# Attention and a gated feed-forward in one kernel: the odd 64 tokens of the first token group move into the second group's product buffers

## The chip, the cores and the metric

The kernel runs on one core of a Trainium2 chip. The metric is the device time of one execution in microseconds (us), the median of several runs.

## The reference, cut to what matters

```python
# q, k, v: (8, 8, 576, 64), float32.  x: 4608 tokens of 512 channels
q_s = softmax(q, axis=-1)               # over the 64 channels of a head
k_s = softmax(k, axis=2)                # over the 576 positions
kv  = einsum('bhsd,bhse->bhde', k_s, v)
x   = einsum('bhsd,bhde->bhse', q_s, kv)   # then (4608, 512)
a, b = x @ w1, x @ w2                   # 512 -> 1024 each
h   = (a * b) @ w3                      # 1024 -> 1024
out = h @ w_out                         # 1024 -> 512
```

No non-linearity stands between `w3` and `w_out`, so the kernel multiplies those two once (`W3O`, 1024 x 512) and the token work is: attention, the products `a` and `b`, their elementwise product, and a third product with `W3O`.

## The kernel before, in words

**Units of work.** Attention runs batch by batch (8 batches of 576 tokens, each in two halves of four heads). Its result is written, transposed, into `xt` (channels on partitions, tokens along the row). The 4608 tokens are cut into six groups for the feed-forward: `GROUPS = [(0, 576), (576, 576), (1152, 1024), (2176, 640), (2816, 1024), (3840, 768)]`. A group has 8 feature blocks `fb` of 128 rows of the 1024 features; each ends in one buffer `ab` (128 x 1024, float16) that holds `a * b` for the group's tokens. There are 18 `ab` buffers, and they are also used at the start for casting `w3` and `w_out`.

**Group 0** takes `plain`: for each `fb` the tokens are cut in two parts (`cut`: 256 and 320 tokens), and `plain_part` issues, for each part, four matmuls for `a` (tasks `pa0`, `pa1`, two each) and four for `b` (`pb0`, `pb1`) at line 591, a copy of `a` to float16 (`pac`, ScalarE or VectorE, line 344) and a multiply (`pm`, VectorE, line 605). **Groups 1 to 5** take `wino`, which gets the two products out of seven half-size products (tasks `x1` to `x4`, `v1`, `v2`, `w`, two matmuls each at line 648) with sums made before (`t_comb`, line 626) and after (line 672, and a multiply at line 699).

**The third product** is `s2`: for a tile of 128 tokens, eight matmuls of 512 columns accumulate over the features (line 739, four tasks of two), then an eviction (line 725 or 727) and two stores of 64 tokens each. Groups 0 and 1 hold 576 tokens, four tiles and 64 tokens more. Those two remainders share one output tile in `s2_ends` (line 759): sixteen matmuls whose stationary operand has 64 columns, eight for the upper half of the output from group 0's buffers and eight for the lower half from group 1's. So all eight `ab` buffers of group 0 are read once more when group 1 is done. Group 4 makes most of its third product by `s2_halves`, the same seven-product scheme (line 836); it needs combinations of `W3O` (`t3_comb`, line 790), which lie in two `st` buffers.

**Loads.** All inputs come through nine `st` buffers (128 x 1152, float32), issued by SyncE (line 310) in the order of the schedule: first `w3` and `w_out`, then q, v and k of the first batch mixed with the rest of them, then `w1` and `w2` in eight pieces, then the other batches. A load waits until the buffer's last reader is done.

**What sets the order.** Every step is a `Task` with a number. Three tables at the head of the file fix everything: `ORDER` (the order in which tasks are emitted, and with it the order on each engine; entries such as `('ps', 7, 9)` are nine filler matmuls that keep TensorE running, line 931), `SLOTS` (which buffer of its pool each use takes) and `ENGS` (which engine takes a task that could run on several). They are the output of a planner that is not part of the file.

Of the kernel before, what the change touches and what calls it, by code (L numbers as in the profile page):

```python
# [18 lines left out]
    ('ps', 7, 9), 6, 12, 4, 14, 1, 10, 3, 2, 96, 0, 97, ('ps', 7, 2), 120, 121, ('ps', 7, 2), 88, 89,  # L19
    ('ps', 7, 3), 90, 128, 98, 5, 129, ('ps', 7, 4), 122, 8, 130, 68, 123, 112, 131, 99, 91, 69, 113, 124,  # L20
    15, 114, 100, 7, 80, 92, 9, 115, 13, 116, 72, 81, 132, 82, 73, 70, 74, 83, 133, 11, 104, 84, 16, 101,
    93, 17, 75, 152, 18, 76, 20, 153, 105, 77, 106, 85, 125, 154, 107, 71, 108, 155, 109, 19, 156, 78, 157,
    134, 144, 21, 86, 142, 145, 94, 79, 126, 143, 87, 102, 140, 95, 117, 146, 135, 110, 103, 147, 160, 136,
    118, 158, 137, 127, 111, 148, 22, 150, 119, 149, 24, 162, ('ps', 7, 3), 151, 23, 164, 139, 163, 138,
    171, 168, ('ps', 7, 4), 141, 173, 170, 159, 169, 161, 172, 25, 165, 180, 166, 484, 167, 508, 182, 174,
    177, 176, 472, 178, 496, 179, 478, 175, 490, 502, 466, 509, 473, 510, 485, 479, 181, 486, 467, 497,
    468, 474, 503, 498, 491, 183, 511, 480, 481, 475, 469, 470, 505, 188, 499, 500, 512, 501, 482, 476, 27,
    483, 504, 506, 190, 487, 26, 471, 493, 513, 488, 28, 186, 538, 477, 492, 494, 30, 189, 507, 526, 550,
    31, 527, 539, 29, 528, 551, 540, 514, 489, 36, 556, 532, 495, 184, 515, 552, 533, 516, 529, 194, 534,
    553, 520, 191, 517, 521, 541, 535, 192, 518, 557, 522, 530, 212, 519, 542, 536, 214, 523, 537, 559,  # L30
    524, 543, 554, 531, 185, 544, 525, 547, 1186, 213, 1200, 558, 545, 196, 560, 215, 548, 202, 1207, 216,
    1208, 204, 203, 217, 1201, 200, 555, 1187, 205, 1193, 546, 1194, 206, 197, 561, 1188, 549, 1202, 201,
    207, 1209, 218, 1210, 219, 187, 1189, 198, 1203, 193, 220, 199, 210, 221, 195, 222, 1190, 1204, 32,
    223, 1211, 34, 208, 225, 211, 1195, 1192, 224, 1196, 209, 37, 232, 235, 229, 38, 234, 233, 236, 237,
    226, 33, 230, 231, 598, 227, 1205, 568, 228, 562, 583, 1197, 1213, 581, 563, 596, 582, 566, 1191, 597,
    587, 584, 585, 567, 600, 564, 586, 611, 569, 570, 601, 588, 599, 571, 603, 565, 626, 589, 602, 35, 604,
    590, 573, 591, 42, 605, 627, 572, 592, 593, 574, 606, 244, 594, 613, 630, 607, 612, 595, 576, 1206,
    575, 608, 628, 631, 609, 615, 578, 629, 616, 632, 610, 579, 633, 246, 641, 577, 618, 580, 634, 614,
    617, 39, 619, 643, 243, 636, 642, 635, 658, 620, 621, 1212, 638, 644, 623, 242, 637, 645, 40, 671, 624,
    646, 656, 673, 622, 672, 648, 657, 639, 647, 649, 1228, 247, 640, 238, 675, 677, 625, 676, 660, 674,  # L40
    1229, 650, 651, 245, 661, 678, 653, 288, 1242, 654, 679, 1243, 652, 286, 655, 663, 680, 662, 248, 664,
    681, 683, 239, 249, 682, 1244, 684, 284, 1230, 43, 665, 1221, 659, 1235, 254, 289, 666, 685, 668, 240,
    1222, 669, 256, 250, 287, 252, 670, 1236, 41, 296, 290, 1237, 667, 1199, 291, 251, 1223, 257, 1198,
    1224, 255, 1238, 1225, 1231, 258, 241, 1239, 1227, 1245, 259, 1232, 292, 297, 1226, 294, 253, 264, 295,
    298, 265, 293, 1214, 281, 266, 285, 1215, 267, 280, 299, 271, 268, 44, 273, 260, 300, 262, 272, 47,
    261, 301, 1216, 270, 263, 283, 45, 1217, 269, 1233, 282, 274, 277, 306, 275, 1241, 279, 307, 278, 1246,
    48, 690, 308, 276, 1218, 304, 46, 309, 302, 305, 52, 313, 310, 303, 315, 705, 54, 311, 312, 720, 314,
    688, 319, 316, 321, 750, 317, 318, 692, 320, 691, 686, 722, 721, 707, 687, 330, 696, 693, 694, 706,
    724, 689, 695, 709, 723, 711, 710, 331, 697, 735, 708, 698, 712, 699, 700, 725, 726, 713, 701, 702,
    328, 727, 703, 737, 728, 714, 715, 704, 337, 756, 716, 736, 717, 1182, 730, 751, 729, 739, 718, 754,  # L50
    740, 731, 741, 755, 752, 738, 719, 322, 732, 753, 742, 335, 782, 733, 362, 743, 49, 757, 1240, 744,
    745, 734, 765, 1248, 746, 758, 767, 1247, 766, 329, 747, 323, 780, 50, 748, 769, 61, 759, 760, 749,
    770, 771, 761, 781, 795, 358, 1183, 768, 772, 784, 324, 783, 786, 773, 785, 1270, 796, 775, 336, 326,
    1271, 774, 787, 762, 1184, 776, 53, 788, 799, 1234, 763, 797, 1277, 789, 800, 1278, 359, 338, 327, 790,
    325, 777, 55, 791, 792, 1220, 332, 802, 764, 333, 801, 798, 803, 1249, 778, 1250, 793, 1256, 805, 779,
    334, 1298, 339, 804, 340, 1299, 1251, 806, 1219, 807, 1257, 808, 1279, 794, 1272, 341, 809, 1258, 1273,
    1280, 1274, 1263, 363, 1264, 1265, 1281, 342, 343, 1283, 1266, 360, 345, 57, 1300, 344, 361, 1267,
    1259, 1252, 1260, 1269, 346, 378, 1268, 347, 348, 352, 379, 1275, 353, 812, 349, 1301, 351, 381, 59,
    354, 829, 380, 1276, 350, 355, 810, 861, 357, 830, 831, 60, 811, 356, 859, 814, 832, 860, 813, 833,
    815, 816, 834, 863, 364, 818, 862, 844, 817, 836, 819, 835, 1302, 837, 821, 366, 1284, 838, 820, 845,  # L60
    822, 839, 56, 396, 1285, 840, 1282, 848, 823, 841, 1303, 1286, 849, 842, 846, 51, 1253, 365, 824, 843,
    864, 1304, 826, 889, 825, 865, 1254, 827, 851, 866, 828, 852, 850, 867, 1291, 847, 400, 1185, 854, 853,
    1287, 868, 869, 855, 874, 870, 856, 875, 1292, 890, 1288, 1293, 857, 891, 1290, 367, 858, 871, 878,
    1262, 872, 893, 398, 880, 879, 1289, 894, 895, 892, 373, 876, 58, 881, 877, 896, 882, 1312, 873, 897,
    368, 1294, 883, 371, 369, 919, 898, 899, 372, 920, 901, 886, 402, 923, 902, 1305, 1295, 887, 904, 903,
    374, 924, 370, 884, 905, 1319, 399, 888, 375, 921, 900, 1306, 885, 376, 1255, 908, 401, 397, 910, 926,
    909, 925, 922, 927, 1320, 403, 911, 1321, 928, 912, 377, 929, 404, 906, 405, 930, 409, 931, 914, 913,
    1313, 407, 932, 916, 915, 395, 1333, 917, 1314, 907, 406, 1326, 933, 1327, 918, 410, 1328, 1322, 408,
    1261, 1315, 1323, 411, 1334, 412, 394, 1335, 1316, 385, 382, 387, 1329, 384, 386, 413, 383, 391, 388,
    392, 393, 998, 390, 389, 414, 999, 63, 415, 1330, 1318, 1000, 416, 62, 1336, 417, 1001, 66, 421, 418,  # L70
    64, 1307, 422, 419, 420, 1308, 1325, 423, 936, 427, 424, 1324, 428, 938, 425, 426, 1317, 1015, 429,
    934, 939, 1013, 1332, 443, 940, 935, 1296, 953, 1014, 937, 942, 1002, 941, 943, 1017, 1003, 1016, 945,
    944, 954, 946, 1005, 1004, 947, 1006, 948, 438, 1007, 957, 950, 949, 958, 1008, 436, 951, 1010, 960,
    1009, 67, 952, 955, 1297, 1011, 961, 959, 439, 963, 434, 1018, 1019, 1309, 956, 1020, 1337, 1012, 962,
    968, 1021, 1339, 1045, 437, 969, 965, 1331, 1340, 431, 1022, 1043, 65, 1023, 430, 964, 1310, 1025,
    1342, 445, 966, 1028, 1311, 1044, 1026, 972, 967, 974, 440, 973, 1024, 1047, 1029, 970, 1027, 1046,
    1048, 1030, 971, 435, 975, 441, 444, 1050, 1032, 976, 446, 983, 1033, 989, 977, 432, 1049, 1031, 1344,
    442, 1051, 978, 447, 980, 984, 1052, 1035, 448, 981, 1338, 987, 1036, 1034, 979, 988, 1053, 433, 1037,
    990, 982, 1038, 1054, 449, 991, 450, 1039, 993, 1346, 992, 1040, 994, 451, 1341, 995, 453, 985, 452,
    1345, 1041, 454, 457, 455, 1055, 996, 456, 1343, 458, 986, 460, 459, 463, 1092, 462, 1056, 461, 1077,  # L80
    464, 1062, 997, 465, 1064, 1042, 1063, 1356, 1058, 1078, 1079, 1057, 1093, 1068, 1059, 1376, 1060,
    1081, 1348, 1066, 1082, 1352, 1096, 1067, 1349, 1084, 1357, 1353, 1069, 1065, 1360, 1355, 1080, 1070,
    1358, 1350, 1361, 1072, 1097, 1363, 1354, 1359, 1099, 1364, 1351, 1362, 1347, 1380, 1365, 1366, 1071,
    1368, 1061, 1367, 1085, 1374, 1369, 1073, 1074, 1373, 1375, 1083, 1075, 1378, 1370, 1377, 1087, 1100,
# [151 lines left out]
def kernel(  # L236
# [11 lines left out]
    nc = tc.nc  # L248
# [716 lines left out]
```

The softmax here doesn't subtract the row's maximum and nothing guards it: scores larger than these inputs give would overflow.

## Time and profile before

| | |
|---|---|
| median of 6 runs | 231.44 us (230.94 to 232.38) |
| profiled execution | 232.04 us, of which the span in the profile is 230.2 us |
| granted TensorE clock | 1.0 throughout |
| TensorE matmul busy | 220.1 us (96%) |
| VectorE busy | 183.5 us (80%) |
| ScalarE busy | 142.1 us (62%) |
| GpSimd busy | 100.9 us (44%) |
| bytes moved | 50.92 MB, of which 38.80 MB are read from HBM |

The profiled execution is one run; 1.8 us of its time lie outside the span. Busy times of matmuls are modelled ends: a matmul's row lasts from its start to its result, and the next one starts long before that, so what a matmul costs is read from the distance of starts (a stretch of x matmuls in the chain, divided by x), not from its mean duration.

### The profile page before, as it was taken

How to read it: one execution, taken by the hardware profiler on the slowest of the kernel's cores; microseconds unless marked ns; L12 is line 12 of the kernel's file. 1: busy time of each engine (PE TensorE's matmuls, PEld its weight loads, DVE VectorE, ACT ScalarE, POOL GpSimd, SP SyncE). 2: the span in 40 equal slices, each digit the busy share in tenths (PEclk: the TensorE clock that was granted, in tenths of full speed). 3: DMA queues.
4: the chain of work that ended last, by engine and by line, in shares of the span. 5: the costliest groups of instructions: out<-in, count | busy, mean ns of one | idle time of the engine just before them, and what ended most of it. 6: DMA issues, size and time to landing. Idle time of an engine off the chain costs nothing.

```text
span 230.2 us, 5284 instructions
## 1 busy us (share of the span) xinstructions
PE 220.1 (96%) x1971; PEld 124.5 (54%) x1971; DVE 183.5 (80%) x392; ACT 142.1 (62%) x289; POOL 100.9 (44%) x84
## 2 busy tenths in 40 slices
PE   7899999999999999999999989999999999999992
PEld 2454448865676564444445656543444367766640
DVE  0432975789999988999967989999999999889820
ACT  2335965768768998777527658765799474354021
POOL 3322545584064990197940368800299920310000
PEclk9999999999999999999999999999999999999999
DMA  6999997980997669819786976669885702124556
GB/s 238 393 405 391 390 387 253 381 325 16 370 374 309 159 234 351 324 29 341 197 190 170 279 276 171 128 106 298 277 213 152 78 0 48 23 68 92 116 132 164
DMA packets 32888, 50.92 MB, mean 221 GB/s; under 512 B 11744, under 2 KB 12000, under 8 KB 32864
## 3 DMA queue, kind: packets, MB, share of 16 engines
q1 hardware_dynamic: 31504, 48.57, 66.6%
q10 hardware_dynamic: 1360, 2.03, 3.7%
q8 instruction: 15, 0.25, 0.4%
q14 instruction: 9, 0.07, 0.1%
HBM read 38.80 MB, written 9.44 MB: 210 GB/s over the span
## 4 chain that ended last, share of the span: by engine, by line
PE 76%; DVE 9%; DMA 8%; ACT 3%; SPq 2%; issue 1%; DVEq 0%; ACTq 0%
PE ps L648 38%; PE ps L739 19%; PE ps L591 7%; PE ps L836 5%; DMA st<-in_q_dram 4%; DMA st<-in_moe_w_out_dram 4%; PE ps L556 2%; PE ps L511 2%; DVE ds L459 2%; SPq L310 2%; DVE tt L626 2%; DVE cc L672 1%; PE ps L485 1%; DVE eq L469 1%; DVE xt L344 1%
## 5 line engine op out<-in xcount | busy, mean ns | idle before, releaser
L672 DVE TENSOR_TENSOR cc<-ps,uu 128x512 f16<-128x512 f32 (+3 forms) x120 | 65.1, 569 | 2.8 <-PE ps L648 0.7
L344 ACT COPY uu<-ps 128x512 f32<-128x512 f32 (+3 forms) x107 | 50.5, 501 | 25.8 <-PE ps L648 14.7
L699 POOL TENSOR_TENSOR ab<-cc,cc 128x512 f16<-128x512 f16 (+3 forms) x25 | 23.1, 927 | 70.4 <-DVE cc L672 59.6
L739 PE MATMUL ps<-W3O,ab 128*128 128x512 f16 (+1 forms) x224 | 53.4, 372 | 0.0
L648 PE MATMUL ps<-tt,wc 128*128 128x512 f16 (+3 forms) x240 | 52.1, 334 | 0.3
L648 PEld LDWEIGHTS <-wc 128*128 128x128 f16 x320 | 30.9, 98 | 25.6 <-DVE tt L626 1.4
L648 PE MATMUL ps<-xt,w 128*128 128x512 f16 (+3 forms) x160 | 36.6, 334 | 0.8 <-ACT osb L725 0.7
L648 PEld LDWEIGHTS <-w 128*128 128x128 f16 x240 | 22.6, 97 | 18.4 <-issue 2.1
L739 PEld LDWEIGHTS <-ab 128*128 128x128 f16 x224 | 21.4, 98 | 20.1 <-issue 0.6
L469 POOL TENSOR_TENSOR eq<-eq,ds 128x1152 f16<-128x1152 f16 x13 | 28.0, 2154 | 5.8 <-DVE ds L466 4.2
L725 ACT ACTIVATE osb<-ps 128x512 f32<-128x512 f32 (+1 forms) x24 | 13.3, 566 | 22.5 <-PE ps L739 19.9
L459 DVE TENSOR_REDUCE ds<-eq 128x9 f32<-128x576 f16 x32 | 23.4, 742 | 4.2 <-ACT eq L455 4.2
L672 DVE TENSOR_TENSOR ab<-ps,cc 128x512 f16<-128x512 f32 (+3 forms) x40 | 22.4, 566 | 1.8 <-PE ps L648 0.6
L455 ACT ACTIVATE eq<-st 128x576 f16<-128x576 f32 x32 | 21.6, 686 | 1.8 <-DMA st<-in_q_dram 1.7
L434 ACT ACTIVATE ek<-st 128x576 f16<-128x576 f32 x32 | 21.0, 686 | 1.9 <-DMA st<-in_k_dram 1.6
L344 ACT CAST xt<-ps 128x320 f16<-128x320 f32 (+7 forms) x46 | 15.2, 398 | 9.4 <-PE ps L556 9.1
L648 PE MATMUL ps<-xt,wc 128*128 128x512 f16 (+3 forms) x80 | 20.2, 334 | 0.0
L648 PE MATMUL ps<-tt,w 128*128 128x512 f16 (+3 forms) x80 | 19.7, 334 | 0.0
L591 PE MATMUL ps<-xt,w 128*128 128x320 f16 (+1 forms) x128 | 16.2, 286 | 0.0
L377 PE MATMUL ps<-ab,ab 128*128 128x512 f16 x64 | 14.8, 379 | 0.4 <-ACT ab L344 0.3
L591 PEld LDWEIGHTS <-w 128*128 128x128 f16 x128 | 12.3, 98 | 3.6 <-issue 0.2
L344 POOL CAST ab<-st 128x1024 f16<-128x1024 f32 x6 | 6.2, 1041 | 15.0 <-DMA st<-in_moe_w_dram 9.1
(76 smaller groups left out, 257.4 us busy)
## 6 DMA issues: line engine op xcount, KB each, us to landing
st<-in_q_dram SPq DMA_DIRECT2D x16, 576.0 KB, 5.8
st<-in_v_dram SPq DMA_DIRECT2D x16, 576.0 KB, 7.5
st<-in_k_dram SPq DMA_DIRECT2D x16, 576.0 KB, 6.4
st<-in_moe_w_dram SPq DMA_DIRECT2D x16, 512.0 KB, 9.0
out_dram<-osb SPq DMA_DIRECT2D x56, 128.0 KB, 3.8
st<-in_moe_w_out_dram SPq DMA_DIRECT2D x4, 512.0 KB, 7.6
out_dram<-osb ACTq DMA_DIRECT2D x14, 128.0 KB, 2.4
out_dram<-osb ACTq DMA_DIRECT2D x3, 64.0 KB, 2.6
```

Source lines behind the costliest of these rows:

```text
L344: {"DVE": nc.vector.tensor_copy, "POOL": nc.gpsimd.tensor_copy, "ACT": nc.scalar.copy}[eng](out=o, in_=i)
L377: nc.tensor.matmul(pp.tile, lhsT=wT.tile[:, gt * P:(gt + 1) * P], rhs=wo[i][1].tile[:, (gt % 2) * C:(gt % 2 + 1) * C], start=(gt == 0), st ...
L434: nc.scalar.activation(out=ek.tile[:, :, j, :], func=AF.Exp, in_=vk(bk.tile)[:, j].rearrange("p (r d) -> p r d", r=RK))
L455: nc.scalar.activation(out=eq.tile[:, :, j, :], func=AF.Exp, in_=vq(bq.tile)[:, j].rearrange("p (r d) -> p r d", r=RK))
L459: nc.vector.tensor_reduce(out=ds.tile[:, 0, j], axis=AX.X, op=ALU.add, in_=eq.tile[:, :, j, :])
L469: {"POOL": nc.gpsimd, "DVE": nc.vector}[e].tensor_tensor(out=eq.tile, in0=eq.tile, op=ALU.mult, in1=ds.tile[:, 1].rearrange("p j r -> p r ...
L591: nc.tensor.matmul(ps.tile[:, 0:m], lhsT=w[qt][:, ct, fo:fo + P], rhs=x[:, ct, lo:lo + m], start=(ct == 0), stop=(ct == 3))
L648: nc.tensor.matmul(ps.tile[:, 0:h], lhsT=lhs(c), rhs=rhs(c), start=first and c == 0, stop=c == 1, skip_group_check=not first)
L672: return lambda: nc.vector.tensor_tensor(out=dst(), in0=ps.tile[:, 0:h], in1=other.tile[:, 0:h], op=op)
L699: {"POOL": nc.gpsimd, "DVE": nc.vector}[e].tensor_tensor(out=ab.tile[:, 0:h], in0=c11.tile[:, 0:h], in1=c21.tile[:, 0:h], op=ALU.mult)
L725: nc.scalar.activation(out=o(), in_=i(), func=AF.Copy, scale=ISC)
L739: nc.tensor.matmul(po.tile[:, :w], lhsT=ab_buf[(g, ft)].tile[:, tb * P:(tb + 1) * P], rhs=W3O[:, ft, m * w:(m + 1) * w], start=(ft == 0), ...
```

## The change

The last 64 tokens of group 0 are no longer a remainder of their own. `plain` cuts group 0 in 512 and 64 tokens, and the product of the 64 is written to columns 576 to 639 of the `ab` buffer that group 1 will use for the same feature block. That buffer is taken already in `plain`, and `wino` of group 1 picks it up. Group 1 then has five full tiles of 128 rows for the third product, of which the last stores half to group 0's tokens; `s2_ends` is gone.

Two more things change. The combinations of `W3O` for group 4 move out of the `st` buffers: two into a new buffer `twx`, two into the first halves of the `w2` weights after their last use; the `st` pool shrinks from nine buffers to eight. And `ORDER`, `SLOTS` and `ENGS` are new tables throughout, since the tasks and the pools are others. (`XCUT` is empty, and the general forms of `rest` and `rows` give the same tiles for groups 2 to 5 as before.)

```diff
+    twx = konst.tile([P, 2, 4, C // 2], F16, name="twx")
-    tiles("st", 9, [P, 2 * RK * D], F32)
+    tiles("st", 8, [P, 2 * RK * D], F32)
...
     def plain(g, fb):
-        ab = buf("ab")
+        ab = ab_buf.get((g, fb)) or buf("ab")
...
         cut = [n * m // parts // 64 * 64 for m in range(parts + 1)]
+        if ENDS and g == 0:
+            ab_buf[(1, fb)] = buf("ab")
+            cut = [0, n - 64, n]
...
     def plain_part(g, fb, qt, fo, ab, lo, m):
+        end = ENDS and g == 0 and lo
+        to, at = (ab_buf[(1, fb)], GROUPS[1][1]) if end else (ab, lo)
+
         def mul():
-            nc.vector.tensor_tensor(out=ab.tile[:, lo:lo + m], in0=pb.tile[:, 0:m], in1=a16.tile[:, 0:m],
+            nc.vector.tensor_tensor(out=to.tile[:, at:at + m], in0=pb.tile[:, 0:m], in1=a16.tile[:, 0:m],
                                     op=ALU.mult)
...
     def wino(g, fb, tb, ts):
-        c11, c22, c21, ab = buf("cc"), buf("cc"), buf("cc"), buf("ab")
+        c11, c22, c21 = buf("cc"), buf("cc"), buf("cc")
+        ab = ab_buf.get((g, fb)) or buf("ab")
...
     def s2(g, tb, parts=1):
...
+        ends = ENDS and g == 1 and at[1] == GROUPS[1][1]
+        if ends:
+            tok = (tok[0], GROUPS[0][0] + GROUPS[0][1] - 64)
...
-    def s2_ends(g0, g1):
-        po, osb = buf("ps"), buf("osb")
...
-                    for m, g in enumerate((g0, g1)):
-                        e = GROUPS[g][1]
-                        nc.tensor.matmul(
-                            po.tile[64 * m:64 * m + 64, :], lhsT=ab_buf[(g, ft)].tile[:, e - 64:e],
-                            rhs=W3O[:, ft], start=(ft == 0), stop=(ft == N_FT - 1))
...
     def t3_comb():
-        bufs = [buf("st"), buf("st")]
...
+        spent = [t for t in plan.tasks if t.name[0] in ("pb0", "wc0", "wc2")]
...
-        if g == 1 and GROUPS[g][1] % P:
-            s2_ends(0, 1)
...
+        if g == 1 and ENDS:
+            rest = [0, 1, 2, 3, (GROUPS[1][1] - 64, GROUPS[1][1])]
```

## The prediction

> **What bounds the kernel now.** I read the page's slices first, to see which engine is never idle and until when the start lasts.
>
> ```profile
> PE   7899999999999999999999989999999999999992
> DVE  0432975789999988999967989999999999889820
> DMA  6999997980997669819786976669885702124556
> ```
>
> A slice is 5.8 us. The DMA engines are full through the first six slices, TensorE nearly always, VectorE from the ninth on. A full digit for TensorE does not say that matmuls follow each other without holes, so next I read the chain of waits in order of time, and take matmul spacing from its long pieces.
>
> ```profile
> 14.36 8.82 DMA st<-in_q_dram
> ...
> 32.58 0.72 PE ps L591 x4
> ...
> 33.84 14.48 PE ps L591 x118
> ...
> 49.99 3.88 PE ps L739 x18
> ...
> 84.07 0.98 PE ps L759 x8
> ...
> 87.83 0.64 DVE xt L344
> ...
> 225.69 0.60 ACT osb L725
> ```
>
> The chain has four parts. Until 32.58 us loads and the first batch's attention; from there to 225.69 us TensorE work (193.1 us); then 4.5 us of eviction and store. In the middle, at 76 to 92 us, the chain runs over VectorE pieces: TensorE waits there in small bits, while it passes from group 1 to group 2.
>
> The spacing of matmuls: 3.88 / 18 = 0.2156 us for 512 columns with a full 128x128 stationary operand; 14.48 / 118 = 0.1227 for the equal mixture of 256 and 320 columns in group 0. The narrowest full one is the transpose at line 485, 128 columns. The forms of TensorE, and one stretch of the timeline:
>
> ```profile
> L591 PE MATMUL ps<-xt,w 128*128 128x320 f16 x64 | 11.8, 299 | 0.0
> L591 PE MATMUL ps<-xt,w 128*128 128x256 f16 x64 | 9.7, 272 | 0.0
> L485 PE MATMUL ps<-ident,eq 128*128 128x128 f16 x72 | 5.7, 219 | 0.4 <-DVE eq L469 0.4
> L759 PE MATMUL ps<-W3O,ab 128*64 128x512 f16 x16 | 2.1, 385 | 0.0
> ```
>
> ```profile
> 83.39 0.68 PE L485 MATMUL ps<-ident,eq 128*128 128x128 f16 x9
> ...
> 86.05 0.11 PEld L648 LDWEIGHTS <-w 128*128 128x128 f16 x2
> ```
>
> Nine transposes take 0.68 us, the last one's own 0.219 included: (0.68 - 0.219) / 8 = 0.0576 us each. Between 128 and 512 columns the spacing thus grows by (0.2156 - 0.0576) / 384 = 0.00041 us a column. With these spacings the counts of the forms table after 32.58 us come to: 432 of 512 columns 93.1; 112 of 384, 176 of 320, 112 of 288 and 192 of 256 together 77.2; line 759 2.0; 54 transposes 3.1; seven batches of 72 small ones at line 511, 0.70 each, 4.9; 15 sets of line 556 at some 0.40, 6.0. That is 186.3 of 193.1 us: only about 7 us are lost to waits after the start. That is the ceiling for any better order.
>
> **The change part by part.** *Group 0's products.* 128 matmuls of 256 and 320 columns (128 x 0.1227 = 15.7 us) become 64 of 512 (64 x 0.2156 = 13.8) and 64 of 64 columns, each with a full weight load. No row shows 64 columns with a full load. Lower bound: the line through the two rows gives 0.0576 - 64 x 0.00041 = 0.031 us. Upper bound: the 128-column row, 0.0576, since the load is the same. The sum is 15.8 or 17.5 us, so +0.1 or +1.8. I take 0.031, because the last row above shows two full weight loads within 0.11 us while one takes 0.098: they follow each other after some 0.012 us, so the load is not what spaces matmuls.
>
> The Trainium skill ("TensorE: Matmul & The Clock Gate", Back-to-back issue gap) speaks against this change: it holds that in a stream of weight loads and matmuls both set the spacing, and gives about 81 ns at 128 columns where this trace has 57.6. By the page's figure the 64 narrow matmuls would take 5.2 us, an estimate, and the change would cost over 3 us here; the row decides, and the sum goes without it.
>
> *Its evictions.* The same number, 16 copies and 16 multiplies. VectorE's multiply took 0.475 and 0.415 us for 320 and 256 columns, 0.681 for 512; for 64 the nearest rows are 0.224 (the 128x64 multiply at line 522) on VectorE and 0.222 (the 128x64 cast) on ScalarE. Per block 0.905 for 0.890, eight times 0.015 = 0.1 us on VectorE, which is 8.0 of 10 us busy in 40 to 50 us. Nothing on the path; +0.1 if that cover were gone.
>
> *The shared tile.* Sixteen half-width matmuls run in pairs: 8 in 0.98 us, 16 in 2.0. Eight full ones take 8 x 0.2156 = 1.7. Gain 0.2 us, on TensorE's path: nearly nothing, since the halves already ran side by side.
>
> *Fillers.* 20 instead of 27, all before the first product, where TensorE waits: 0.
>
> *The load buffer.* At the start the DMA engines are full (1.04 and 1.05 of 16 engines in 10 to 30 us, some 390 GB/s). The first `w1` piece remains the 19th load, behind the same bytes. Eight buffers could leave a hole of at most one buffer, 0.59 MB / 390 GB/s = 1.5 us; on the other side the last q load goes up by one place (one `w3` piece, 0.52 MB, 1.3 us earlier), and the chain above runs through it. I take 0, between -1.3 and +1.5. Later the reads have room: 38.8 MB are 99 us at that rate, and what stands behind a late load on SyncE's queue are stores of third-product tiles, which nobody but their own four buffers awaits. `t3_comb` now waits for the last use of `w2`; group 4's third product, its only reader, comes 90 us after `w2`'s loads, and `pb0` and the `wc` sums are over by then.
>
> *The `ab` buffers, and the order.* Before, group 0's eight buffers are held until its remainder is read (line 759, ending 85 us); with group 1's eight only 2 of 18 are free for group 2, and all of group 1's third product stands ahead of group 2's first product on TensorE. After, group 0's buffers are free after its four tiles. The new order uses that: behind group 2's first product stand two whole tiles of group 1 (16 matmuls, 3.45 us) that TensorE can do while VectorE makes `xt` and the sums of line 626. What was lost there is read from the window:
>
> ```profile
> 76.20:92.00 15.80, 15.52 (x267) 8.31 (x265) 14.10 (x34) 14.60 (x32) 9.14 (x7) 1.00 0.82 267
> ```
>
> Its 267 matmuls by their spacings: 35 of 512 columns 7.5, 36 transposes 2.1, line 759 2.0, 144 small ones 1.4, four sets of line 556 1.5 (at 0.37, the pieces that waited least), 4 of 288 columns 0.5: 15.0 of 15.8 us; at the 0.22 that two pairs of 256 columns need, 14.4. So 0.8 to 1.4 us can be had here. A stall that goes lets VectorE be late next: it is 14.1 of 15.8 us busy here, and its work is the same. The other passages (120 to 134, 150 to 161, 177 to 186 us) have new orders too, with 1.7 us of group 3's tiles behind group 4's first product where 1.3 were; I see no sign for either side there and put -1.0 to +1.5 (the holes counted at 177 to 186 us come to about 0.8, the largest of the three). For order and buffers together I take -1.2, the middle of what this passage holds and nothing for the others, between -1.4 - 1.0 = -2.4 and +1.5.
>
> Sum: +0.1 - 0.2 - 1.2 = -1.3 us. The profiled execution (232.04, of which span 230.2) would become 230.7; it was 0.6 above the median 231.44, so on the median's scale 230.1.
>
> **The rivals.** *Same time:* VectorE gets the freed time and is late next. For it: VectorE is at 9 or more tenths for most of 45 to 200 us, and its work by counts and rows changes by about 1 us of 175 (seven evictions of third-product tiles leave it, copies at the start come). Then only +0.1 - 0.2 remains: 231.4. *Slower:* the 64-column products are spaced by their weight load, at 0.0576 instead of 0.031 us, 64 x 0.027 = +1.7, with no gain elsewhere: 233.0. It decides from a spacing of some 0.05 us on, where 64 x 0.019 = 1.2 eats the gain. For it: no row shows a full load with so little work behind it; against it: the two loads in 0.11 us. A late load at the start, with the first product at 34 us instead of 32.6, would give the same sign. *It does not do what it says:* for TensorE's work this is nearly so, 0.2 us, and it is in the sum.
>
> **How the numbers follow.** Faster by over 0.3% (0.7 us, about what a measurement of this kernel can tell from no change): the gain at the passage holds, and spacing stays under 0.045: 0.47. Within it: 0.18. Slower, by the narrow products, the load buffers or a passage that the new order makes worse: 0.35. All gains at their ends give 231.44 - 1.3 - 2.4 - 0.1 = 227.6, all losses 231.44 + 1.8 + 1.5 + 1.5 = 236.2; neither is likely whole. The range takes the likeliest case's lower half and the slower rival: 228.4 to 233.3.
>
> **What would show it.** Line 591's 64-column form: starts 0.03 or 0.06 us apart. The first product at 32.6 us, within 1 us. Line 739's rows among line 648's where group 2 begins, and holes of TensorE there under 0.5 us. It would be wrong if the first product came after 34 us, if line 591's work took over 17 us, or if the 7 us of holes after the start grew.

## The result and the profile after

| | before | after |
|---|---|---|
| median | 231.35 us (37 runs) | 232.84 us (18 runs, 231.50 to 234.65) |
| ratio | | 1.0065, 95% interval [1.0046, 1.0083] |
| profiled execution | 232.04 us, span 230.2 | 233.09 us, span 231.3 |

The change makes the kernel slower by about 1.5 us; 230.1 was forecast. The page's slices of the kernel after, then its chain of waits in order of time:

```profile
PE   7699979999999989999999999999999989999991
DVE  0444876889899998999997899869999999987600
POOL 1110550849635996043530367710498833300300
DMA  6999997994997866096947979859948000224275
```

```profile
32.48 1.04 PE ps L597 x4
33.89 12.13 PE ps L597 x90
...
61.39 0.74 DVE cc L686 x2
62.68 1.15 PE ps L662 x8
64.78 2.25 PE ps L662 x16
...
76.29 2.19 POOL v L345 x2
...
79.86 1.80 POOL eq L470
81.91 2.17 POOL eq L470
84.12 0.68 PE ps L486 x9
```

The first product starts where it did (32.48, before 32.58). New is GpSimd: before, no piece of it stood in the middle of the chain; now two casts of `v` and the `eq` normalisations carry it from 76 to 84 us. Two windows, each first of before, then of after (length, then busy us of TensorE, its loads, VectorE, ScalarE, GpSimd with their instructions; last granted clock, DMA share, GB/s):

```profile
34.00:55.00 21.00, 21.00 (x156) 14.86 (x155) 15.88 (x35) 13.83 (x26) 11.89 (x6) 1.00 0.76 274
55.00:92.00 37.00, 36.51 (x498) 22.89 (x496) 33.95 (x84) 31.84 (x73) 19.04 (x15) 1.00 0.81 280
```

```profile
34.00:55.00 21.00, 21.00 (x160) 10.75 (x157) 17.13 (x35) 12.14 (x24) 11.68 (x7) 1.00 0.88 303
55.00:92.00 37.00, 34.71 (x476) 21.40 (x474) 34.65 (x85) 30.63 (x69) 26.63 (x20) 1.00 0.80 264
```

Group 0's products are done without an idle moment in both. From 55 to 92 us TensorE is busy 1.8 us less and GpSimd 7.6 us more. What TensorE waits for there, from the table of waits (us, times, longest):

```profile
PE ps L486 <- POOL eq L470: 0.8, 1, 0.8
PE ps L662 <- DVE cc L686: 0.5, 1, 0.5
```

To count finely I take from the trace the distance between starts of neighbouring matmuls, less the spacing that the first one's shape needs (216 ns at 512 columns, 136 at 320, 109 at 256, 56 at 128, 29 at 64). What is left over, the holes, in us of one profiled execution each; "end" is from the last matmul's start to the end of the span:

| kernel | to 34 | 34-55 | 55-70 | 70-92 | after 92 | end |
|---|---|---|---|---|---|---|
| before | 6.78 | 0.03 | 1.45 | 2.46 | 6.18 | 4.91 |
| before, new `ab` slots (control) | 6.63 | 0.04 | 1.46 | 2.10 | 5.32 | 4.88 |
| after | 8.02 | 0.10 | 2.66 | 3.56 | 4.87 | 5.23 |
| uneven cut alone | 7.46 | 1.59 | 1.45 | 1.79 | 5.49 | 4.92 |
| move with even cut | 6.43 | 0.07 | 1.46 | 2.13 | 6.01 | 4.91 |
| last (`f4_no_race`) | 7.33 | 0.62 | 1.73 | 3.41 | 4.87 | 5.64 |

After against before: +1.24 at the start, +0.07, +1.21, +1.10, -1.31 behind 92 us, +0.32 at the end; TensorE's own work is 1.51 us less (207.17 to 205.65). Together +1.1, the difference of the spans. The 1.51 us are the seven filler matmuls fewer (20 for 27, 7 x 0.216), and fillers all lie before 34 us. So the +1.24 at the start is no loss: fillers have become idle time, and without them TensorE had done 0.3 us more work by 34 us than before (1.51 less 1.24). What the kernel after loses lies in the two passages, 55 to 92 us (+2.3), and at the end. The profiled execution of before lies 0.7 above its median; the control beside it shows a usual one, against which the passages lose more (1.2 and 1.5) and the gain behind 92 us is 0.45. The control, the uneven cut alone and the move with the even cut have 27 fillers, the last kernel 20.

### The profile page after: what moved, and what is told of

Read it like the earlier page. It is cut to its first block, busy times and chain, and to the rows that moved or that the text cites. A ratio compares the mean times of both kernels' runs of the same rounds, so it can differ in the third digit from the quotient of the medians.

```text
span 231.3 us, 5259 instructions
## 1 busy us (share of the span) xinstructions
PE 218.2 (94%) x1956; PEld 119.3 (52%) x1956; DVE 185.5 (80%) x395; ACT 143.3 (62%) x289; POOL 99.7 (43%) x81
## 4 chain that ended last, share of the span: by engine, by line
PE 70%; DVE 10%; DMA 6%; POOL 6%; issue 5%; ACT 1%; SPq 0%; DVEq 0%; ACTq 0%; POOLq 0%
PE ps L662 36%; PE ps L766 17%; PE ps L597 6%; PE ps L836 5%; DMA st<-in_q_dram 4%; POOL eq L470 3%; DVE cc L686 3%; PE ps L557 2%; DMA st<-in_moe_w_dram 2%; PE ps L512 2%; DVE tt L639 2%; DVE ds L460 1%; DVE xt L345 1%; PE ps L486 1%; POOL ab L713 1%
## 5 line engine op out<-in xcount | busy, mean ns | idle before, releaser
L766 PE MATMUL ps<-W3O,ab 128*128 128x512 f16 (+1 forms) x232 | 57.8, 372 | 0.0
L662 PE MATMUL ps<-tt,wc 128*128 128x512 f16 (+3 forms) x240 | 52.8, 334 | 0.8 <-DVE tt L639 0.6
L662 PEld LDWEIGHTS <-w 128*128 128x128 f16 x240 | 22.7, 98 | 18.8 <-DVE cc L686 1.3
L739 ACT ACTIVATE osb<-ps 128x512 f32<-128x512 f32 (+1 forms) x30 | 16.7, 570 | 19.4 <-PE ps L766 13.7
L456 ACT ACTIVATE eq<-st 128x576 f16<-128x576 f32 x32 | 21.1, 687 | 5.9 <-DMA st<-in_q_dram 5.9
L662 PE MATMUL ps<-xt,wc 128*128 128x512 f16 (+3 forms) x80 | 19.5, 334 | 0.0
L597 PE MATMUL ps<-xt,w 128*128 128x512 f16 (+1 forms) x128 | 17.6, 286 | 0.7 <-DVE w L345 0.7
L345 ACT CAST xt<-ps 128x256 f16<-128x256 f32 (+7 forms) x42 | 14.3, 407 | 5.6 <-PE ps L557 5.5
L597 PEld LDWEIGHTS <-w 128*128 128x128 f16 x128 | 8.8, 98 | 9.6 <-DVE w L345 0.8
L345 POOL CAST v<-st 128x1152 f16<-128x1152 f32 x10 | 11.4, 1147 | 5.2 <-DMA st<-in_v_dram 2.8
```

The lines of the kernel that those rows point to most:

```text
L345: {"DVE": nc.vector.tensor_copy, "POOL": nc.gpsimd.tensor_copy, "ACT": nc.scalar.copy}[eng](out=o, in_=i)
L456: nc.scalar.activation(out=eq.tile[:, :, j, :], func=AF.Exp, in_=vq(bq.tile)[:, j].rearrange("p (r d) -> p r d", r=RK))
L597: nc.tensor.matmul(ps.tile[:, 0:m], lhsT=w[qt][:, ct, fo:fo + P], rhs=x[:, ct, lo:lo + m], start=(ct == 0), stop=(ct == 3))
L662: nc.tensor.matmul(ps.tile[:, 0:h], lhsT=lhs(c), rhs=rhs(c), start=first and c == 0, stop=c == 1, skip_group_check=not first)
L739: nc.scalar.activation(out=o(), in_=i(), func=AF.Copy, scale=ISC)
L766: nc.tensor.matmul(po.tile[:, :w], lhsT=rows(ab_buf[(g, ft)].tile), rhs=W3O[:, ft, m * w:(m + 1) * w], start=(ft == 0), stop=(ft == N_FT - 1))
```

## Experiments: old order and new order

"Old order" means the orders and engines of before, carried over to the changed kernel's tasks by their names. Theory A: the new tables are to blame; B: the eight load buffers; C: the data path (cut, narrow products, `ab` buffers taken early).

**The move of the 64 tokens alone**, in the old order.

```diff
 # before, with plain, plain_part, wino, s2 of after; ORDER and ENGS of before
     tiles("st", 9, [P, 2 * RK * D], F32)
```

> Only the data path of the change (512 and 64 tokens in group 0, the 64 in group 1's buffers, a full fifth tile, no shared tile), in the order and with the engines of the kernel before, nine load buffers, and the combinations of W3O in load buffers as before; only the ab buffers are dealt out anew. Theory A, the new tables are to blame: within 0.3% of the kernel before, some 231.2 to 231.6 us. Theory B, the eight load buffers are to blame: the same. Theory C, the narrow products or the early taken ab buffers are to blame: slower by 1 us or more, 232.5 us.

234.05 us, ratio 1.0118 [1.0095, 1.0141].

**The changed kernel with nine load buffers**, new order.

```diff
-    tiles("st", 8, [P, 2 * RK * D], F32)
+    tiles("st", 9, [P, 2 * RK * D], F32)
```

> The changed kernel with its new tables and nine load buffers instead of eight (the ninth holds the two combinations of W3O once the loads have left it; only the load buffers are dealt out anew). Theory A: no faster than the changed kernel by more than 0.3 us, 232.5 to 233 us. Theory B: the loads between 35 and 56 us come earlier, the holes at 55 to 68 us shrink and 1 to 1.5 us come back, 231.4 us. Theory C: as A.

233.01 us, 1.0096 [1.0060, 1.0132]: the buffer gives nothing back in the new order.

**The whole change in the old order** (eight buffers; a load moves back in the order until a buffer is free).

```diff
 # after, with ORDER and ENGS of before
```

> The whole change (eight load buffers, the combinations of W3O in their new places), in the order and with the engines of the kernel before; three loads stand a little later in the order because a buffer must be free, and the load and ab buffers are dealt out anew. Theory A: within 0.3% of the kernel before, 231.2 to 231.8 us. Theory B: slower by 1 to 1.5 us, 232.5 us or more. Theory C: slower by 1 us or more, and e1 too.

234.76 us, 1.0141 [1.0118, 1.0164]. So the tables aren't to blame for all of it: without them the change costs 3.4 us, with them 1.5. A falls in its plain form, C stands.

**Old order up to entry 650** (middle of group 2), **new behind it**, and the reverse.

```diff
 # after: ORDER = old[:650] + what is left, as in new     (e4)
 # after: ORDER = new[:650] + what is left, as in old     (e8)
```

> The whole change with eight load buffers; the order and engines of the kernel before up to the steady middle of group 2 (650 of 1480 entries, the same work but for two dozen tasks done by then in both), the new order and engines from there. By the holes counted on TensorE the new order loses 3.2 us more than the old one before 93 us and 1.3 us less after it. Theory A: faster than the kernel before by about 1 us, 230.2 us. Theory B: the start pays for the buffer, 231.5 us or more. Theory C: 232 us.

> The counterpart of the fourth run: the whole change, in the new order up to the middle of the second group and in the old order from there. The fourth run (old, then new) took 233.26, the whole change in the old order 234.76 and the changed kernel 232.84, so the new order won 1.5 us behind the middle and 0.4 ahead of it. If the two stretches add up, this one takes 234.3 us, ratio 1.011 to 1.016. If the stretches depend on each other (the new order's first stretch pays for its second), it takes over 235 or under 233.5.

Old, then new: 233.26 us, 1.0090 [1.0069, 1.0110]. New, then old: 235.27 us, 1.0179 [1.0135, 1.0224]. The stretches don't add up; an order's second half pays for how its first half leaves the queues. Buffers of several pools had to be dealt anew at the seam, so these two assign nothing by themselves.

## Experiments: the cut

**The uneven cut alone**, in the kernel before.

```diff
         cut = [n * m // parts // 64 * 64 for m in range(parts + 1)]
+        if g == 0:
+            cut = [0, n - 64, n]
```

> The kernel before with one line more: the first group's 576 tokens are cut into 512 and 64 for the plain products instead of 256 and 320. Nothing is moved behind the second group, the order and the engines are those of before. It asks whether the uneven cut by itself costs what the first four runs left open (the move of the 64 tokens in the old order was +2.9 us, ratio 1.0118). Theory D, the uneven cut is the cost (one eviction of 512 columns holds a PSUM buffer and VectorE or ScalarE twice as long as one of 256, and the 64-column products behind it give TensorE nothing to cover that): 233 to 234 us, ratio 1.008 to 1.013, with the extra holes of TensorE between 32 and 53 us. Theory E, the shared ab buffers are the cost (the second group's buffers are taken already while the first group is made, since the 64 columns of the first group go into them, so fewer are free): 231.2 us, ratio 0.998 to 1.003. The narrow-product rival of the prediction (a 64-column product is spaced by its weight load) would also show here, at about +1.7 us; the spacing of those products in this trace tells it from D.

233.01 us, 1.0065 [1.0043, 1.0087]: this one line costs 1.7 us. Its forms:

```profile
L593 PE MATMUL ps<-xt,w 128*128 128x512 f16 x64 | 15.6, 379 | 0.5 <-DVE ab L607 0.3 <-DVE xt L344 0.2
L593 PE MATMUL ps<-xt,w 128*128 128x64 f16 x64 | 5.0, 193 | 0.0
L607 DVE TENSOR_TENSOR ab<-ps,cc 128x512 f16<-128x512 f32 x8 | 5.3, 682 | 1.0 <-PE ps L593 1.0
L607 DVE TENSOR_TENSOR ab<-ps,cc 128x64 f16<-128x64 f32 x8 | 1.5, 210 | 2.6 <-PE ps L593 2.6
```

The narrow products start 29 ns apart (median), so it isn't their spacing. The multiplies take 6.8 us together, as the even ones did (3.6 + 3.2). What changes is who waits when: VectorE waits 2.6 us for narrow products, and TensorE waits for the wide multiplies, as here:

```profile
40.56 2.15 DVE L607 TENSOR_TENSOR ab<-ps,cc 128x512 f16<-128x512 f32 x5 [0.27 <-PE ps L593]
41.90 1.02 PE L593 MATMUL ps<-xt,w 128*128 128x512 f16 x4 [0.29 <-DVE ab L607]
```

The holes from 34 to 55 us grow from 0.03 to 1.59, and those ahead by 0.7: the first 512-column product needs twice the tokens of `xt`, and a hole of 0.40 at 34.16 waits for one.

**The move with the even cut**, old order, nine buffers: 256 and 320 as before, the second multiply split.

```diff
-            cut = [0, n - 64, n]
...
-            nc.vector.tensor_tensor(out=to.tile[:, at:at + m], in0=pb.tile[:, 0:m], in1=a16.tile[:, 0:m],
+            nc.vector.tensor_tensor(out=ab.tile[:, lo:lo + r], in0=pb.tile[:, 0:r], in1=a16.tile[:, 0:r],
                                     op=ALU.mult)
+            if end:    # r = m - 64
+                nc.vector.tensor_tensor(out=to.tile[:, at:at + 64], in0=pb.tile[:, r:m],
+                                        in1=a16.tile[:, r:m], op=ALU.mult)
```

> The same move of the 64 tokens as in the first run (old order, nine load buffers, the shared fifth tile full), but the first group's tokens stay cut into 256 and 320 as before; the last multiply that writes the 320 columns is split in two, 256 into the first group's ab buffer and 64 into the second group's. So the ab buffers are taken as early as in the first run, while the cut is even; VectorE has eight small multiplies more (about 0.5 us of its time, from rows of 0.06 us for such a one). Theory D (the uneven cut): the cost goes away, 231.0 to 231.8 us, ratio 0.998 to 1.003. Theory E (the ab buffers taken early): it stays, 233.5 to 234.5, ratio 1.009 to 1.015. Half and half, about 232.5, would leave both standing.

231.24 us, 0.9990 [0.9972, 1.0008] (the eight small multiplies took 0.21 us each, not the 0.06 of the expectation). The whole cost of the first run is gone with the cut; sharing the tile and taking the `ab` buffers early cost nothing that can be measured, and bring nothing. D holds, E falls, in the old order.

**Control: new `ab` slots in the kernel before.**

```diff
 # before: SLOTS of the ab pool dealt to the slot free for longest
```

> A control: the kernel before, with the ab buffers' slots dealt anew by the rule that was used in the runs with the old order (the slot free for longest), and nothing else changed. If the new deal is what those runs paid for, this one is 2 us or more slower (ratio over 1.008); if not, it stays within 0.3% of before, 230.7 to 231.9 us, which theories D and E both expect.

231.00 us, 0.9978 [0.9963, 0.9993]: the deal is not what was paid.

**A cut between.**

```diff
-            cut = [0, n - 64, n]
+            cut = [0, n - 192, n]
```

> The kernel before with the first group cut into 384 and 192, everything else as it was: a cut between the even one (256 and 320: ratio 1) and the uneven one (512 and 64: 1.0065). If the cost follows the length of the longest eviction (475 ns at 320, about 551 at 384, 682 at 512), it is 231.7 to 232.0, ratio 1.002 to 1.003. If it comes only with the very narrow part, whose four matmuls are over in 0.12 us while its two evictions take 0.43, it stays at 231.0 to 231.5, ratio 0.998 to 1.001.

231.54 us, 1.0010 [0.9996, 1.0024]; its holes from 34 to 55 us are 0.55. Between the two expectations.

**The casts on ScalarE**, with the uneven cut and, as control, without.

```diff
 # ENGS: all 16 tasks pac of group 0
-    "DVE" (6 of them)
+    "ACT"
```

> The kernel with the uneven cut alone (ratio 1.0065), with all 16 casts of the first group's products on ScalarE; six of them were on VectorE (2.3 us of its time in that stretch, from rows of 692 and 222 ns). If the cost of the cut lies in VectorE's queue, where a cast stands ahead of the multiply that frees the next PSUM buffer, it goes down by 0.7 us or more, to 232.3 or less. If it lies in the length of the chain matmul, cast, multiply whoever does the cast, it stays at 232.7 to 233.3; ScalarE was busy 13.6 of 23 us there and can take the casts.

> The control of the run beside it: the kernel before with the same six casts on ScalarE. If the place of the casts is of no weight with the even cut, 231.0 to 231.7, ratio 0.998 to 1.002.

233.05 us, 1.0079 [1.0056, 1.0101], and 231.21 us, 1.0003 [0.9986, 1.0020]. Relieving VectorE of 2.3 us of casts doesn't help, so its load is not what costs. What is left is the chain from a wide product over cast and multiply to the free PSUM buffer, in an order made for shorter ones; no run shortened that chain by itself.

**The even cut in the new order**, the changed kernel otherwise.

```diff
-            cut = [0, n - 64, n]
...
 # and the split multiply as above; six s2 steps 2 to 8 places later
```

> The changed kernel, in its new order and with its eight load buffers, but with the first group cut into 256 and 320 as before and the multiply of the 320 part split in two (256 columns into the first group's ab buffer, 64 into the second group's). Six steps are put later by 2 to 8 places of the order, since they now read both parts. So it differs from the changed kernel (ratio 1.0065) in the cut alone. Theory D, the uneven cut is the whole cost: 230.5 to 231.5 us, ratio 0.995 to 1.001. Theory H, the new order costs something too, which the cut does not explain (its holes at 60 to 90 us, 4.6 us against 2.2 before, come from VectorE's and GpSimd's new order): 232 to 233, ratio 1.003 to 1.007.

237.84 us, 1.0273 [1.0234, 1.0313]. Neither theory: an even cut is far worse in an order made for the uneven one (holes of 2.03 from 34 to 55 us, 5.65 from 55 to 70). This order doesn't fit the even cut, while the old one took 384 and 192 at no cost that can be measured. That puts the run with the uneven cut in its place, too: its 1.7 us are best read as the price of that cut in an order made for another one, and, so far as it lies at 34 to 55 us, the changed kernel doesn't pay it: it has 0.10 us of holes there.

**The even cut with eight buffers**, old order, and with the new order behind entry 650.

```diff
 # after, even cut as above; ORDER = old                                   (e13)
 # after, even cut as above; ORDER = old[:650] + what is left, as in new   (e12)
```

> The whole change in the old order with eight load buffers and the even cut of the first group; it differs from the run with nine buffers (231.24, ratio 0.999) in the buffer alone. With the uneven cut the buffer was worth 0.7 us. If that is a price of its own, 231.9 us, ratio 1.001 to 1.004; if the ninth buffer is not needed where nothing else is late (the prediction's term of 0), 231.2, ratio 0.998 to 1.000.

> The fourth run (whole change, old order up to the middle of the second group, new order behind it, eight load buffers; ratio 1.009) with the first group cut evenly into 256 and 320, the multiply of the 320 part split in two. Old order and even cut fit each other in the first stretch. Theory D (an uneven cut in an order made for the even one is what the old order paid, and the new order is better behind the middle): 3 us less than the fourth run, 229.9 to 230.7 us, ratio 0.993 to 0.998, faster than both kernels. Theory J (the new order's gain behind the middle was only a repair of what the uneven cut had broken ahead of it): 231 to 232, ratio 0.999 to 1.003.

231.83 us, 1.0019 [1.0006, 1.0031], against 0.9990 with nine buffers: 0.6 us, as in the old order with the uneven cut (0.7). But the last matmul starts no later (224.35 us, with nine 224.45); the 0.6 lie behind the last eviction. DMA queues from the last eviction's end on, first of the kernel with nine buffers, then of this one:

```profile
core 0 of [0], span 229.4 us
...
q1 hardware_dynamic: 230, 0.37, 35.8%
...
out_dram<-osb ACTq DMA_DIRECT2D x1, 128.0 KB, 2.8
```

```profile
core 0 of [0], span 230.0 us
...
q1 hardware_dynamic: 231, 0.37, 29.9%
...
q14 instruction: 1, 0.01, 0.9%
...
out_dram<-osb ACTq DMA_DIRECT2D x1, 128.0 KB, 3.6
```

An 8 KB read of instructions (0.69 us long in the trace) falls beside the last store, which lands 0.8 us later. This goes with the place of the `W3O` combinations, not with the number of buffers: in all eight kernels with them in `st` no such read lies between the last eviction and the end, and the span ends 3.84 to 3.88 us after that eviction; in all twelve with them in `twx` and the `w2` weights (one has nine `st` buffers) it ends after 4.09 to 4.65 us, and in ten of these such a read starts between 0.1 us before and 2.7 us after the eviction. In one of the other two no read is there and the end is late all the same (4.23), so that the read delays the store is likely, and not shown.

The second, with the new order behind entry 650: 231.92 us, 1.0025 [1.0009, 1.0041]; the new order's second half brings nothing where the first half fits.

## Experiments: the new order's passages

**A weight sum to GpSimd.** TensorE's hole at 64.78 us stands behind these, of the kernel after:

```profile
62.67 1.15 POOL L345 CAST v<-st 128x1152 f16<-128x1152 f32 x1
```

```profile
62.76 1.59 DVE L396 TENSOR_TENSOR wc<-w,wc 128x1024 f16<-128x1024 f16 x1
64.28 0.81 DVE L686 TENSOR_TENSOR cc<-ps,uu 128x288 f16<-128x288 f32 x2
```

```diff
 # ENGS: the last weight sum, and group 1's combination tt4
-    195: "DVE", 565: "POOL",
+    195: "POOL", 565: "DVE",
 # ORDER: 195 directly ahead of 565
```

> The changed kernel with two steps exchanged between VectorE and GpSimd in its order: the last weight sum (two operations, 1.59 us on VectorE at 62.76 in the midst of the second group's evictions; about 4.25 on GpSimd at 2.12 each) goes to GpSimd, ahead of the combination there, and that combination (1.43 on GpSimd) goes to VectorE (0.46). If the new order's holes are the loss, the holes at 62.68 (0.28) and 64.78 (0.64) go, and the time falls by 0.4 to 0.9 us, to 232.0 to 232.4, ratio 1.003 to 1.005. If other waits take their place (the passage to the third group waits for GpSimd at 84.12 anyway, 0.94), it stays at 232.8, ratio 1.005 to 1.008.

234.48 us, 1.0146 [1.0104, 1.0188], worse by 1.6. (The expectation took the sum for two operations; it is one, and long.) Its trace shows why:

```profile
59.38 2.33 POOL L393 TENSOR_TENSOR wc<-w,wc 128x1024 f16<-128x1024 f16 x1
59.84 2.19 DVE L636 TENSOR_TENSOR tt<-tt,xt 128x576 f16<-128x576 f16 x1
```

A combination on VectorE that takes 0.46 us elsewhere lasts 2.19, until GpSimd's sum is over. The sum at 62.76 above is of the same kind: 1.59 instead of 0.68, beside GpSimd's cast.

**That collision taken away from either side.**

```diff
 # ORDER: task 195 (VectorE's sum) behind 590, two evictions later            (f2)
 # ORDER: task 285 (GpSimd's cast) behind 595, one load held back for it      (f3)
```

> The changed kernel with one step moved in VectorE's order: the last weight sum (1.59 us at 62.76, 0.68 when nothing is beside it) stands behind the two evictions that followed it. If the collision with GpSimd's cast and the place ahead of the evictions make the holes at 62.68 and 64.78, they shrink by 0.5 to 0.9 us, and the time is 231.9 to 232.4, ratio 1.002 to 1.005. If the time is given back at the next passage (GpSimd's normalisation at 84.12), it stays at 232.8, ratio 1.005 to 1.008.

> The changed kernel with GpSimd's cast of a value part (1.15 us at 62.67) put behind its second addition of the second group, so that it no longer runs beside VectorE's sum; VectorE's order stays as it is, and one load of the fourth batch is held back, since that cast frees its buffer. If the collision alone makes VectorE late, its sum takes 0.68 us instead of 1.59, the hole at 64.78 (0.64) goes, and the time is 232.0 to 232.5, ratio 1.003 to 1.005. If the place of the sum is what counts, nothing changes: 232.8.

232.69 us, 1.0084 [1.0048, 1.0120], and 233.72 us, 1.0083 [1.0053, 1.0112]. No gain in time. Yet in the second the sum takes 0.68 us and the hole behind it is gone:

```profile
64.28 0.68 DVE L393 TENSOR_TENSOR wc<-w,wc 128x1024 f16<-128x1024 f16 x1
```

Its twelve runs fall into two groups, 231.66 to 232.22 (5) and 233.70 to 234.40 (7), so neither its median nor its ratio is that of a usual run. The profiled one is of the upper group, and has another collision:

```profile
39.70 2.12 POOL L393 TENSOR_TENSOR wc<-w,w 128x1024 f16<-128x1024 f16 x1 [5.40 <-ACT w L342]
39.93 2.44 DVE L342 CAST w<-st 128x1024 f16<-128x1024 f32 x1
42.42 0.82 PE L594 MATMUL ps<-xt,w 128*128 128x512 f16 x3 [1.42 <-DVE w L342]
```

In the kernel after, VectorE came first, by 0.26 us, and it was GpSimd that waited:

```profile
40.02 0.68 DVE L345 CAST w<-st 128x1024 f16<-128x1024 f32 x1
40.28 2.40 POOL L396 TENSOR_TENSOR wc<-w,w 128x1024 f16<-128x1024 f16 x1 [5.31 <-ACT w L345]
```

GpSimd's start hangs on a cast on ScalarE that waits for a load; that cast starts at 38.57 here and at 39.16 in the kernel after. So a load some tenths of a microsecond earlier turns VectorE's short cast into a long one. The same long cast stands in two more profiled executions, each in the upper group of its kernel's runs: 2.54 us at 39.84 with nine buffers in the new order (234.86; four of its six runs are at 232.64 to 233.13), and 1.83 at 40.93 with the sum later (235.13; five of eight at 232.15 to 232.95).

**The race taken away.**

```diff
 # as the last kernel, and ENGS: the cast w1c (1, 1)
-    190: "DVE",
+    190: "ACT",
 # ORDER: 190 directly behind 188
```

> The last kernel (GpSimd's cast later) with one step more moved: the cast of a weight part that VectorE does at 39.93 goes to ScalarE, ahead of ScalarE's own two. Then nothing on VectorE races with GpSimd's sum at 39.7. If that race makes the two times, there is one time left, the lower: 231.5 to 232.3, spread under 1 us, ratio 1.000 to 1.004, and the 1.4 us hole of TensorE at 42.4 is gone. If the two times come from something else (the reads, the clock), they stay: about 232 and 234. What is left above the kernel before then is the price of the rest of the new order and of the eighth buffer.

232.34 us, 1.0073 [1.0049, 1.0096]. The hole at 42.4 us is gone, and no run is above 233.6; but two of six are at 233.45 and 233.59, four at 231.92 to 232.44. The expectation of one narrow group is missed: those two have a lower granted clock (0.989, the four others 0.996 to 0.998), which the kernel before this one had in only three of its seven upper runs (0.987 and 0.988), so what the race and what the clock does to the two groups isn't separated. And the ratio is not measurably below those of the two kernels before it. So the collisions are there, and their removal mends their holes, but they are not the bulk of the 1.5 us. What this last kernel still has above the control is in the table: 1.3 us at 70 to 92 us, where TensorE waits for GpSimd's normalisation as in the kernel after (a hole of 0.92), 0.8 at the end and 0.6 at 34 to 55 us. Its 0.7 more before 34 us are less than the 1.5 of the seven fillers, so it starts earlier (first product at 31.80).

No version of the change beats the kernel before by more than its interval.

## Why the prediction was wrong, point by point

**Right.** The first product at 32.48 us (forecast 32.6), and no price at the start: the holes before 34 us that are more, 1.24 us, are less than the seven fillers' 1.5. The narrow products: 29 ns apart, forecast 31; the slower rival, spacing by the weight load, is out, though 233.0 was its time. The two forms:

```profile
L597 PE MATMUL ps<-xt,w 128*128 128x512 f16 x64 | 15.7, 379 | 0.7 <-DVE w L345 0.7
L597 PE MATMUL ps<-xt,w 128*128 128x64 f16 x64 | 4.7, 193 | 0.0
```

The Trainium skill's figure of 81 ns at 128 columns ("TensorE: Matmul & The Clock Gate", Back-to-back issue gap) doesn't hold here; this trace has 56, and 29 at 64 columns. The shared tile's 0.2 us is within what the move with the even cut leaves open (0.9972 to 1.0008).

**The step that failed: "The `ab` buffers, and the order", -1.2 us.** The passage at 76 to 92 us was to gain by two whole tiles of the third product behind group 2's first product. They stand behind it, but behind the waits too:

```profile
82.75 0.59 PE L662 MATMUL ps<-xt,w 128*128 128x512 f16 x2
84.12 0.68 PE L486 MATMUL ps<-ident,eq 128*128 128x128 f16 x9 [0.78 <-POOL eq L470]
...
92.10 0.59 PE L766 MATMUL ps<-W3O,ab 128*128 128x512 f16 x2
```

Their sixteen matmuls start at 92.10 to 101.38, and the passage's large holes (0.94, 0.35 and 0.37 us) all end by 85.8. TensorE takes them in the order of the table, and a tile covers a wait only where it stands ahead of the matmul that waits. In the passage there are now 12 matmuls of the third product, where there were 17 and the 16 of line 759; before, no hole in it was above 0.30 us. No run moved the two tiles forward, so how much they would have covered is not shown. The window now:

```profile
76.20:92.00 15.80, 14.60 (x254) 7.83 (x253) 14.90 (x37) 13.03 (x27) 13.26 (x10) 1.00 0.73 222
```

TensorE's 15.52 us have become 14.60, and GpSimd's 9.14 are 13.26; 3.2 of these 4.1 us are two combinations (line 639), of which it made none here before. I read what stands behind the product on TensorE's queue, and not what stands ahead of the normalisation on GpSimd's and VectorE's. First before, then after:

```profile
78.34 4.25 POOL L469 TENSOR_TENSOR eq<-eq,ds 128x1152 f16<-128x1152 f16 x2 [0.32 <-DVE ds L466]
82.54 1.15 POOL L344 CAST v<-st 128x1152 f16<-128x1152 f32 x1
...
79.83 0.27 DVE L466 RECIPROCAL ds<-ds 128x18 f32<-128x18 f32 x1
```

```profile
75.56 0.73 POOL L713 TENSOR_TENSOR ab<-cc,cc 128x288 f16<-128x288 f16 x1
76.23 2.24 POOL L345 CAST v<-st 128x1152 f16<-128x1152 f32 x2
78.43 1.43 POOL L713 TENSOR_TENSOR ab<-cc,cc 128x288 f16<-128x288 f16 x2
79.80 6.49 POOL L470 TENSOR_TENSOR eq<-eq,ds 128x1152 f16<-128x1152 f16 x3
...
79.90 1.41 DVE L460 TENSOR_REDUCE ds<-eq 128x9 f32<-128x576 f16 x2
81.34 0.27 DVE L467 RECIPROCAL ds<-ds 128x18 f32<-128x18 f32 x1
```

Before, one `v` cast stood on GpSimd's queue here, behind two normalisations, at 82.54; now two stand ahead of the three that run in one piece from 79.80, and the transposes at 84.12 wait for the second of these. But the casts are the smaller part of that wait: the divisors of the second one come from VectorE at 81.61, 0.3 us before it starts and 1.5 us later than before (80.10). Without the casts, and with VectorE's order as it is, it could start 0.3 us earlier.

The term should have been +1.1 to +1.5 for 70 to 92 us and +1.2 for 55 to 70, a passage that the sum didn't look at. For the later passages I put -1.0 to +1.5 and took nothing; they gained 0.5 to 1.3. So order and buffers together cost 1.0 us (against the profiled run of before) to 2.2 (against the control), where -1.2 was forecast. The `ab` buffers themselves are neutral. The ceiling was also too low, which changes nothing here: the table has 10.1 us of holes behind 34 us before, not 7, and 11.2 after; that they would grow was named as a sign of being wrong.

**Evictions of group 0, "nothing on the path".** VectorE's work did grow by almost nothing (six evictions of third-product tiles leave it, not seven). But "8.0 of 10 us busy" is no cover: with the work unchanged the cut cost 1.7 us in the order made for the other cut. The new order hides this, and it is part of what the new order is for.

**The load buffer, 0.** It held: the ninth buffer gives nothing back in the new order, and in the old order with the even cut the last matmul starts no later without it. Only in the old order with the uneven cut, where eight buffers cost 0.7 us, the first product came later (33.13 us, with nine 32.13, one profiled run each). What costs 0.3 (after) to 0.8 us, the end, was in no term.

**The start and the fillers** were to be 0, and were, as said. In the old order, where all kernels have 27 fillers, holes before 34 us are 0.4 to 0.9 us more in the profiled runs with the uneven cut than in that of before, while those with an even one or 384 and 192 have 6.4 to 6.7. The wide first product, which needs more of `xt`, would explain that; for the new order this was not tried apart.

**What stays open.** How the 1.5 us split between the place of the two tiles, the collisions, the queues of GpSimd and VectorE, and the end: the table splits one profiled execution, and no run moved the two tiles or took GpSimd's `v` casts at 76 us away. Why the move with the uneven cut costs 1.0 us more than the cut alone, in the old order, also stays open; their profiled spans are alike (231.2 and 231.1), but that of the move is its fastest run (233.29). An order made anew for the moved tail with the even cut wasn't tried.

## What to carry to other kernels

When a change comes with a new schedule, price the schedule on every queue: a gain read off the bottleneck engine's queue says nothing as long as the queues of its suppliers have been dealt anew, and work that is to cover a wait must stand ahead of the instruction that waits. An order is made for certain sizes; an edit of sizes tested in the old order, or the old sizes in the new order, measures misfit (here 0.7% and 2.7%) and not the edit, so try it from both sides. And when the parts of a tile may be cut evenly and the output split instead, try the even cut first: here it left the existing order in peace.

## What the runs showed of the hardware

VectorE and GpSimd can hold each other up where both work from SBUF to SBUF: a combination of 0.46 us took 2.19, a sum of 0.68 took 1.59, a float32 to float16 cast of 0.68 took 2.44, each ending 0.3 to 0.6 us after GpSimd's operation; when VectorE began first, GpSimd's took 2.40 instead of 2.12. Not every operation is held up: VectorE's evictions from PSUM kept their durations beside GpSimd (0.68 at 512 columns), and so did the reductions of line 460, which also go from SBUF to SBUF (0.74 in all 22 that began beside a GpSimd operation in the kernel after). The Trainium skill ("SBUF — State Buffer", SBUF: two separate sides) says that GpSimd shares a pair of ports with VectorE's operations that have two inputs in SBUF or run in a two-port mode, and that it is an exclusive lock for a whole instruction to whoever starts first. The runs agree. Where such a start hangs on a load it becomes a race: in three kernels the profiled execution with the long cast is in the upper of two groups of times some 2 us apart. That the race alone makes the groups is not shown.
